# Block-sparse attention and a squared-ReLU MLP on one core: when six weight blocks are decoded, and how values and spilled outputs are laid out

## The chip, the cores and the metric

The kernel runs on one core of a Trainium2 chip. The metric is the device time of one execution in microseconds. Work is spread over TensorE (PE; its weight loads are shown apart as PEld), VectorE (DVE), ScalarE (ACT), GpSimd (POOL) and SyncE (SP), which here only issues transfers. Each engine takes its instructions in the order in which they were written for it and waits by semaphores for the others.

## The reference

`q`, `k` and `v` are 4 batches × 8 heads × 768 positions × 64 features in float32. Attention is masked by blocks of 32 positions, and its output is the input of an MLP over all 3072 tokens:

```python
scores = scale * np.matmul(q, k.transpose(0, 1, 3, 2))
mask = np.abs(blk_i - blk_j) <= window              # window = 1, blocks of 32
mask = mask | (blk_i == 0) | (blk_j == 0) | (blk_i == n_blocks - 1) | (blk_j == n_blocks - 1)
for qb in range(n_blocks):
    for kb in sampled_blocks[qb]:                   # 3 random blocks per row of blocks
        mask[qb * block:(qb + 1) * block, kb * block:(kb + 1) * block] = True
scores = np.where(mask, scores, -1000000000.0)
attn = np.exp(scores - np.max(scores, axis=-1, keepdims=True))
attn = attn / (np.sum(attn, axis=-1, keepdims=True) + 1e-09)
x = np.matmul(attn, v)                              # then heads side by side: 3072 x 512
h = x @ w_in                                        # 512 x 2048
r = np.maximum(h, 0.0)
out = (s * (r * r) + b) @ w_out                     # 2048 x 512
```

The weights reach the device as raw 64-bit words, so the kernel turns each of them into two float32 parts itself.

## The kernel before, in words

Attention goes slot by slot. A dense slot (`aD0` to `dD1` in the list `ORD`) is the first and last block of queries of one batch for four heads: two units of work. A sparse slot (`0A1` to `1C6`, 44 of them) is one row of blocks of a *pair* of batches for all heads: four units. The pairs are batches 0 and 1, called a and b, and batches 2 and 3, called c and d. There are 52 slots and N = 192 units. Units 0 to 99 are almost all of the first pair, 100 to 191 almost all of the second. Per unit PE forms scores (L914 dense, L936 sparse), DVE takes the maximum (L953), ACT the exponential (L965), PE transposes (L990), DVE or ACT copies the result out of PSUM (L1001, L1003), PE multiplies with the values (L1022 dense, L1033 sparse), DVE scales (L1039), PE transposes again (L1045), ACT copies (L1050), and SP spills the slot's output to a DRAM tensor `xd` (L1057 sparse, L1061 dense). On PE the scores of a slot stand two slots ahead of its product with the values.

Keys of a pair lie in one large tile (`kt0`, `kt1`); POOL copies the blocks that a sparse slot needs into `kk` (L873 to L886). Values of sparse slots are loaded by SP, slot by slot, into `vA` and `vB` (L765 window, L858 sampled). Values of dense slots are loaded by `load_v` into tiles `z0` and `z1`: 128 columns of all 768 rows of a batch per load, two loads a slot, 16 in all (L729). Afterwards `z0` and `z1` hold the split input of the MLP.

The 32 blocks of weights (16 of `w_in`, `i0` to `i15`, and 16 of `w_out`, `o0` to `o15`) go through the same decode, `decode_f64`: SP loads 512 KB into one of three staging buffers `kraw` (L57), DVE masks and combines (L75, L77, L78), ACT takes sign and magnitude (L79, L81, L82), and DVE writes the high part (L83) and the low part (L84, L85) where the block has its home. The homes of the first six blocks in the list `WL` (`i0 o0 i1 o1 i2 i3`) lie in `kt0`, the keys' tile of the first pair. The three staging buffers also take the MLP's first inputs, read back from `xd` by `xload` (L386) and split by ACT and DVE (`xsplit`, L399 and L401).

After attention come 30 plain MLP steps: `mlp1` (L426 to L428), `relu`, `square`, `hidden_high`, `hidden_low` (L431 to L447), `mlp2` (L468 to L470), each for a group of 384 tokens and one block of 128 hidden features. They run while the rest of the weights is decoded. Then the remaining batches use a scheme with seven products in place of eight (L605), for which DVE prepares sums of weights and inputs (L563 to L589).

The order of all this, up to the preparation of the seven products, is not written by hand. A class `Plan` holds every step with its engine, an assumed cost, what it depends on, which buffers it takes and uses, and a due number. `Plan.order` plays the engines forward in time: at each point the engine that can start earliest takes, among the steps that could start by then, the one with the smallest due number. Due numbers are in units of attention: a maximum of unit n has n - 26, a copy out of PSUM n - 8, the load of dense values u - 12 where u is the slot's first unit, loads of sampled values u - 13, a spill u - 14. The decode of the k-th block of `WL` has N + 22.5 + 15.5 k, that is 214.5, 230 and so on, its load 4 less, and the reload of the MLP's input N + 6: all of them above every due number of attention, so they are only taken where an engine had nothing of attention to do.

Of the kernel before, what the change touches and what calls it, by code (L numbers as in the profile page):

```python
# [9 lines left out]
F32 = mybir.dt.float32  # L10
# [9 lines left out]
P = 128  # L20
# [3 lines left out]
F64_SHIFT = 8.0 * 0x38000000  # L24
F32_MOST = float(0x7F7FF000)
T = {
# [176 lines left out]
def kernel(  # L203
# [16 lines left out]
    nc = tc.nc  # L220
    B, S, DM = v.shape
# [4 lines left out]
    BLK = 32  # L226
    NPAIR = 4
# [15 lines left out]
    dpool = ctx.enter_context(tc.tile_pool(name="dpool", bufs=1, space=DRAM))  # L243
# [4 lines left out]
    nc.gpsimd.memset(b_top, F32_MOST + F64_SHIFT)  # L248
    b_most = cpool.tile([P, 1], F32, name="b_most")
    nc.gpsimd.memset(b_most, F32_MOST)  # L250
    xd = dpool.tile([B, 2, P, NM, NPAIR, BLK], F32, name="xd")
    wod = dpool.tile([4, P, 2 * DM], F32, name="wod")


# [8 lines left out]
    NBANK = 7  # L263
    RB = 3
# [118 lines left out]

    def xload(g, c2, dst=None):
        t = scratch("kraw", 2 * HALF, f"xraw{g}_{c2}") if dst is None else dst
        nc.sync.dma_start(out=t.rearrange("p (t y) -> p t y", t=NM), in_=xd[g // 2, g % 2, :, :, 2 * c2:2 * c2 + 2, :].rearrange("p t c n -> p t (c n)"))  # L386
        xraw[(g, c2)] = t

    def xsplit(g, c, part=None):
# [259 lines left out]
    with ExitStack() as es:  # L649
        pers = es.enter_context(tc.tile_pool(name="pers", bufs=1))  # L650
        QB = 4
# [49 lines left out]

        vbox = {}

        def dense_values(n):
            if "z0" not in vbox:
                for z in ("z0", "z1"):
                    vbox[z] = gp.tile([P, 4, NCH, P], F32, tag=z, name=f"v{z}", bufs=1)
            return vbox[f"z{n // 4}"][:, n % 4]

        def value_tiles():  # L710
            if "A" not in vbox:
                for z in "AB":
# [7 lines left out]
            value_tiles()  # L720
            return vbox["B"][:, n - 1] if n else vbox["A"][:, NST]

        vst = {}

        def load_v(i, pr):
            kind, b, x, _ = slots[i]
            vt = vst[(i, pr)] = dense_values(len(vst) % 8)
            h0 = (2 * x + pr) * P
            nc.sync.dma_start(out=vt, in_=v[b, :, h0:h0 + P].rearrange("(c p) d -> p c d", p=P))  # L729

        def block_rows(e, j, n=1):

# [283 lines left out]

        def av_dense(i, j):

            xs, vt, pt = out_of(i, j), vst[(i, j)], pts_of.pop(unit_of[i] + j)
            for c in range(NCH):  # L1020
                for rows in halves:
                    nc.tensor.matmul(xs[rows], pt[c // 3][:, c % 3, rows], vt[:, c, rows], start=(c == 0), stop=(c == NCH - 1))  # L1022

        def av(i, j):
            kind, e, k, r = slots[i]
# [26 lines left out]
        def spill(i):  # L1052
            kind, b, k, _ = slots[i]
            xst = xst_of.pop(i)
            if kind == "s":
                hf, m = divmod(k - 1, NM)
                nc.sync.dma_start(out=xd[2 * b:2 * b + 2, hf, :, m].rearrange("a p c n -> p a (c n)"), in_=xst)  # L1057
                return
            x = k
            for m in range(2):  # L1060
                nc.sync.dma_start(out=xd[b, 1, :, NM - 2 + m, 2 * x:2 * x + 2, :],  # L1061
                                  in_=xst.rearrange("p x (a m n) -> p (x a) m n", a=2, m=2)[:, :, m, :])


        plan = Plan({"kraw": RB, "qr": QB, "dv": 8, "z0": 1, "z1": 1, "kk": 1, "kg": KG, "vs": VG, "vg": 2, "B": NBANK,
                     "o": 1, "P": len(ptiles), "pt": 5, "xst": 3, "xss": 2, "nm": 10, "dn": 5,
                     "rc": 5, "wp": 4, **{f"kt{k}": 1 for k in range(B // 2)}})
        op = plan.op
# [45 lines left out]


        pq = pdv = pvl = pvs = pk = o_m = o_e = o_rc = o_ev = None
        spills, tensor, lqs, before, globs = {}, {}, {}, {}, []

        costs = {"s": (530, 470, 265), "d": (810, 350, 780)}
        cols = {"s": (1800, 1024, 500), "d": (1536, 768, 768)}  # L1120
        for i, (kind, e, k, r) in enumerate(slots):
# [4 lines left out]
            if qk not in lqs:  # L1126
                lqs[qk] = {}
                for a in range(2):
                    for par in range(2):
# [4 lines left out]
            lv, av_deps, av_use, s_deps, s_use = {}, [], [], [], [("qr", qk)]  # L1134
            if dense:
                for pr in range(2):
                    new = [] if pdv else [("z0", "dv"), ("z1", "dv")]
                    pdv = lv[pr] = op("s", 450, u + pr - T["DL"], lambda i=i, pr=pr: load_v(i, pr), alloc=[("dv", (i, pr)), *new],
                                      use=[] if new else [("z0", "dv"), ("z1", "dv")], order=[pdv], nbytes=393e3)
                av_use = [("z0", "dv"), ("z1", "dv")]  # L1140
                s_use.append((f"kt{e // 2}", e // 2))
            else:
                prev = before.get(r)
                entire = k == STREAMS[r]
                first = not before
                blocks = [*range(k - 1, k + 2), 0] if entire else [k + 1]
                new = [("kk", "kk")] if first else []
                pk = op("g", 1900 if entire else 430, u - T["GK"], lambda i=i, w=entire: window_k(i, w),
                        [*parts_of(e, blocks), *(prev[0] if prev else [])], alloc=new, use=[(f"kt{e}", e)] + ([] if first else [("kk", "kk")]), order=[pk])
                s_deps.append(pk)  # L1150
                for a in range(NSL):
                    pk = op("g", 430 if a else 700, u - T["GK"] + 0.1 * (a + 1), lambda i=i, a=a: sampled_k(i, a), [o_si, *parts_of(e, range(NB))],
                            alloc=[] if a else [("kg", i)], use=[(f"kt{e}", e), ("kk", "kk")] + ([("kg", i)] if a else []), order=[pk])
                    s_deps.append(pk)
                s_use += [("kk", "kk"), ("kg", i)]

                vt = [("vg", "vA"), ("vg", "vB")]
                if first:
                    for m in range(5):
                        pvl = op("s", 450, u - T["VL"] - 0.5 + 0.1 * m, lambda m=m: global_values(m), alloc=[] if m else vt, use=vt if m else [],  # L1160
                                 order=[pvl], nbytes=(131e3 if m == 4 else 200e3))
                        globs.append(pvl)
                av_deps += globs if e == 0 else []
                for m in range(len(runs(k, entire)) + (entire and e > 0)):
                    pvl = op("s", 450, u - T["VL"] + 0.1 * m, lambda i=i, w=entire, m=m: window_v(i, w, m), prev[1] if prev else [],
                             use=vt, order=[pvl], nbytes=131e3)
# [50 lines left out]
            for j in range(nu):  # L1217
                pts = [("pt", (u + j, g)) for g in range(2)] if dense else [("pt", (u + j // 2 * 2, 0))]
                o = op("p", cost[2], u, lambda i=i, j=j: av(i, j), cols=col[2],
                       deps=[*evs[j], *av_deps, *([lv[j]] if dense else [])],  # L1220
                       alloc=[] if j else [("o", i)],
                       use=[*av_use, *pts] + ([("o", i)] if j else []) + ([("dv", (i, j))] if dense else []))
# [256 lines left out]
```

## Time and profile before

| | us |
|---|---|
| median of 3 runs | 800.08 (799.3 to 804.42) |
| profiled execution, time | 797.14 |
| its span, first to last instruction | 795.4 |
| PE busy | 729.3 (92% of the span) |
| DVE busy | 574.0 (72%) |
| ACT busy | 473.0 (59%) |
| POOL busy | 239.5 (30%) |

The profile is of one execution. Its times count from the first instruction. A busy PE means that a matmul is under way, not that the array is at its peak. "Granted clock" is the share of full speed that TensorE's clock had. Attention ends at about 258 us, the plain MLP steps and the decode of weights last until about 430 us, and the seven-product stage fills the rest.

### The profile page before, as it was taken

To read this page: it belongs to the slowest core of one execution; us is meant where nothing else is said; L and a number is where in the kernel's file an instruction comes from. 1 tells how busy PE (TensorE), PEld (TensorE's weight loads), DVE (VectorE), ACT (ScalarE), POOL (GpSimd) and SP (SyncE) were. 2 spreads that over 40 slices of the span, in tenths; PEclk is the share of its full clock that TensorE was granted. 3 is DMA by queue.
4 is the path that set the end of the run, shared out by engine and by line. 5 is a ranking of instruction groups with operands and counts; after the bars stand their busy time and mean duration, and the time that the engine had idled before them with its cause. 6 is when DMAs were issued, how large, how long until landed. Compare 5 with 4: busy or idle time off the path is not lost.

```text
span 795.4 us, 20754 instructions
## 1 busy us (share of the span) xinstructions
PE 729.3 (92%) x7872; PEld 618.5 (78%) x7872; DVE 574.0 (72%) x1439; ACT 473.0 (59%) x1141; POOL 239.5 (30%) x392
## 2 busy tenths in 40 slices
PE   6678779888889999999889999999999999999997
PEld 5456557666657897888778998998999998989996
DVE  3365667568568899998898678678668778766662
ACT  3365667567678787778874434476455357534542
POOL 6452533453531222221002322232232223222321
PEclk9799999889899999999999999999999999999999
DMA  9978789988787433544542241035000013000002
GB/s 253 241 175 228 206 238 234 242 239 209 179 229 196 141 123 105 170 160 131 137 139 75 87 125 56 33 80 149 12 1 0 1 40 99 1 1 1 1 0 80
DMA packets 118915, 95.80 MB, mean 120 GB/s; under 512 B 50272, under 2 KB 97504, under 8 KB 118816
## 3 DMA queue, kind: packets, MB, share of 16 engines
q1 hardware_dynamic: 116512, 88.18, 40.0%
q0 software_dynamic: 2304, 6.29, 3.1%
q8 instruction: 62, 1.02, 0.6%
q14 instruction: 37, 0.30, 0.1%
HBM read 75.57 MB, written 14.68 MB: 113 GB/s over the span
## 4 chain that ended last, share of the span: by engine, by line
PE 63%; DVE 15%; ACT 8%; DMA 6%; issue 5%; SPq 3%; ACTq 0%; DVEq 0%
PE m L605 19%; PE o L469 8%; PE o L470 8%; PE o L468 8%; PE t L990 6%; PE xs L1033 5%; PE s L936 4%; DMA vA<-in_v_dram 3%; DMA xd<-xst 2%; PE xs L1022 1%; DVE hid L438 1%; DMA qr_0d<-in_q_edge_dram 1%; DVE wkhp L84 1%; PE s L914 1%; ACT hid L442 1%
## 5 line engine op out<-in xcount | busy, mean ns | idle before, releaser
L447 POOL TENSOR_TENSOR hid<-hid,hid 128x384 fp32r<-128x384 f32 x120 | 132.7, 1106 | 410.1 <-ACT hid L623 246.1
L622 ACT ACTIVATE hid<-hid,sb_b,sb_s 128x384 f32<-128x384 f32 x96 | 68.1, 709 | 150.5 <-DVE hid L616 150.5
L965 ACT ACTIVATE ptile<-ptile,nm 128x256 f32<-128x256 f32 (+1 forms) x208 | 107.3, 518 | 46.6 <-DVE nm L953 46.2
L953 DVE CUSTOM_DVE_ANT_1 ptile<-s,mt 128x256 f32<-128x256 f32 x176 | 64.3, 421 | 30.4 <-PE s L936 30.3
L1033 PE MATMUL xs<-vA,pt 128*32 128x64 f32 x1696 | 50.3, 227 | 24.8 <-DMA vA<-in_v_dram 10.9
L1033 PEld LDWEIGHTS xs<-vA,pt 128*32 128x32 f32 x1696 | 37.4, 113 | 45.3 <-issue 13.0
L469 PE MATMUL o<-woutr,hid 128*128 128x512 f32 x168 | 66.9, 398 | 1.0 <-DVE woutr L85 1.0
L468 PE MATMUL o<-woutr,hid 128*128 128x512 f32 x168 | 65.9, 392 | 1.6 <-DVE woutr L83 1.6
L470 PE MATMUL o<-woutr,hid 128*128 128x512 f32 x168 | 66.8, 398 | 0.0
L605 PE MATMUL m<-wout,win 128*128 128x384 f32 x264 | 62.6, 340 | 2.5 <-ACT xrest L1372 1.6
L990 PE MATMUL t<-ident,ptile 128*128 128x128 f32 x448 | 64.2, 290 | 0.4 <-issue 0.4
L605 PE MATMUL m<-xp,wop 128*128 128x384 f32 x288 | 58.3, 337 | 0.0
L469 PE MATMUL o<-win,hid 128*128 128x512 f32 x144 | 56.8, 394 | 0.0
L616 DVE SCALAR_TENSOR_TENSOR hid<-hid 128x384 f32<-128x384 f32 x96 | 54.0, 563 | 3.3
L605 PE MATMUL m<-xp,win 128*128 128x384 f32 x288 | 55.1, 338 | 1.4 <-DVE xp L589 0.7
L990 PEld LDWEIGHTS t<-ident,ptile 128*128 128x128 f32 x448 | 51.2, 147 | 6.6 <-issue 1.7
L605 PEld LDWEIGHTS m<-xp,win 128*128 128x128 f32 x288 | 51.0, 188 | 4.6 <-DVE xp L589 1.2
L623 ACT CAST hid<-hid 128x384 fp32r<-128x384 f32 x96 | 49.4, 515 | 7.5 <-ACT hid L622 0.4
L886 POOL COPY kk<-kt 128x256 f32 x132 | 47.9, 402 | 18.8 <-issue 14.0
L605 PEld LDWEIGHTS m<-xp,wop 128*128 128x128 f32 x288 | 51.5, 188 | 2.1
L605 PEld LDWEIGHTS m<-wout,win 128*128 128x128 f32 x264 | 47.4, 188 | 5.5 <-ACT xrest L1372 2.4
L470 PE MATMUL o<-win,hid 128*128 128x512 f32 x126 | 49.8, 395 | 0.0
(172 smaller groups left out, 1778.4 us busy)
## 6 DMA issues: line engine op xcount, KB each, us to landing
vB<-in_v_dram SPq DMA_DIRECT2D x109, 128.0 KB, 3.6
vA<-in_v_dram SPq DMA_DIRECT2D x75, 128.0 KB, 4.5
raw_i<-in_w_in_dram SPq DMA_DIRECT2D x16, 512.0 KB, 4.0
raw_o<-in_w_out_dram SPq DMA_DIRECT2D x16, 512.0 KB, 3.7
vz<-in_v_dram SPq DMA_DIRECT2D x16, 384.0 KB, 6.2
xd<-xst SPq DMA_DIRECT2D x44, 128.0 KB, 3.8
out_dram<-ob SPq DMA_DIRECT2D x20, 256.0 KB, 2.0
sum<-xd SPq DMA_DIRECT2D x12, 384.0 KB, 4.5
```

The costliest lines, as they stand in the source:

```text
L447: (eng or nc.vector).tensor_tensor(out=htile(5 + i % 3), in0=t, in1=gh.bitcast(F32), op=ALU.subtract)
L468: nc.tensor.matmul(acc, gh[:, tsl], wout(f, 0), start=first, stop=False)
L469: nc.tensor.matmul(acc, gh[:, tsl], wout(f, 1), start=False, stop=False)
L470: nc.tensor.matmul(acc, gl[:, tsl], wout(f, 0), start=False, stop=last)
L605: nc.tensor.matmul(to, w_, x_, start=(c == 0 and k == 0), stop=(c == 1 and k == 2))
L616: vec.scalar_tensor_tensor(out=t, in0=t, scalar=0.0, in1=t, op0=ALU.max, op1=ALU.mult)
L622: nc.scalar.activation(t, t, AF.Identity, bias=sb_b, scale=sb_s)
L623: nc.scalar.copy(gh, t)
L953: nc.vector.tensor_tensor_reduce(out=pt, in0=sp, in1=msk, scale=-scale, scalar=FMAX if g == 0 else nm[:, 0:1], op0=ALU.add, op1=ALU.min, a ...
L965: nc.scalar.activation(pt[:, :w], pt[:, :w], AF.Exp, bias=nms[n][:, last:last + 1], scale=-1.0, accum_out=dns[i][:, g, j:j + 1])
L990: nc.tensor.transpose(tp[:, (2 * j + c) * P:(2 * j + c + 1) * P], src[:, c * P:(c + 1) * P], ident)
L1033: nc.tensor.matmul(xs[quads[pair]], pt[:, c, quads[pair]], vt[:, a, col:col + D], start=(j == 0 and c == 0), stop=(c == 1), tile_position= ...
```

## The change

Four things in the text of the kernel:

- **Weights.** Two new numbers, `WE` = -84 and `WD` = 16. The first six blocks of `WL` get the due number N - 84 + 16 k where that is smaller, that is 108, 124, 140, 156, 172 and 188 instead of 214.5 to 292; their loads have 4 less, as before. The other 26 blocks keep theirs. The steps themselves and their places in memory stay.
- **Dense values.** `load_v` now loads half the rows of a batch, all 512 columns of them, in one transfer of 768 KB whose rows are 2 KB long; two such loads a batch, eight in all instead of 16 of 384 KB with rows of 512 bytes. Batches a and c use `z0`, b and d `z1`, where before eight smaller pieces were spread over both. Both loads have the due number of the batch's first slot, and every product of the batch waits for both.
- **Spills.** `xd` gets another shape, so that the outputs of both batches of a pair stand side by side in it: a sparse spill writes runs of 1 KB instead of two runs of 512 bytes. What reads `xd` back (`xload`) has its addresses changed to match, with runs of the same length as before.
- **First order.** The list `ORD` itself is the same in both kernels. The order in which steps stand on the engines changes only as `Plan` works it out anew from the new due numbers, buffers and sizes.

```diff
-    "WL": "i0 o0 i1 o1 ...", "WP": 22.5, "WS": 15.5, "XP": 16.0, "LOW": 24,
+    "WL": "i0 o0 i1 o1 ...", "WP": 22.5, "WS": 15.5, "WE": -84.0, "WD": 16.0, "XP": 16.0, "LOW": 24,
...
-    xd = dpool.tile([B, 2, P, NM, NPAIR, BLK], F32, name="xd")
+    xd = dpool.tile([B // 2, 2, P, NM, 2, NPAIR, BLK], F32, name="xd")
...
-        def load_v(i, pr):
-            kind, b, x, _ = slots[i]
-            vt = vst[(i, pr)] = dense_values(len(vst) % 8)
-            h0 = (2 * x + pr) * P
-            nc.sync.dma_start(out=vt, in_=v[b, :, h0:h0 + P].rearrange("(c p) d -> p c d", p=P))
+        def load_v(b, half):
+            if ("d", b) not in vbox:
+                vbox[("d", b)] = gp.tile([P, NCH, DM], F32, tag=f"z{b % 2}", name=f"vz{b}", bufs=1)
+            rows, n = slice(half * HALF, (half + 1) * HALF), NCH // 2
+            nc.sync.dma_start(out=vbox[("d", b)][:, half * n:(half + 1) * n], in_=v[b, rows, :].rearrange("(c p) d -> p c d", p=P))
...
-                nc.sync.dma_start(out=xd[2 * b:2 * b + 2, hf, :, m].rearrange("a p c n -> p a (c n)"), in_=xst)
+                nc.sync.dma_start(out=xd[b, hf, :, m].rearrange("p a c n -> p a (c n)"), in_=xst)
...
+                vz = (f"z{e % 2}", ("dv", e))
+                if e not in dvs:
+                    dvs[e] = []
+                    for half in range(2):
+                        pdv = op("s", 450, u - T["DL"] + 0.1 * half, lambda e=e, half=half: load_v(e, half), alloc=[] if half else [vz],
+                                 use=[vz] if half else [], order=[pdv], nbytes=786e3)
+                        dvs[e].append(pdv)
+                av_deps += dvs[e]
+                av_use = [vz]
...
+            wat = N + min(T["WP"] + T["WS"] * k, T["WE"] + T["WD"] * k if k < 6 else 1e9)
...
-            pw = last_load = op("s", 450, N + T["WP"] - 4 + T["WS"] * k, load, [prev_k], alloc=[raw], nbytes=524e3, late=T["LATE"])
+            pw = last_load = op("s", 450, wat - 4, load, [prev_k], alloc=[raw], nbytes=524e3, late=T["LATE"])
...
-                mine[m] = wdone[(which, f, m)] = op(eng, cost[m], N + T["WP"] + T["WS"] * k + 0.3 * m, fn, deps, alloc=alloc, order=order,
+                mine[m] = wdone[(which, f, m)] = op(eng, cost[m], wat + 0.3 * m, fn, deps, alloc=alloc, order=order,
```

More of the change, by code (lines that the diff above doesn't have):

```diff
@@ L385, in xload @@
         t = scratch("kraw", 2 * HALF, f"xraw{g}_{c2}") if dst is None else dst
-        nc.sync.dma_start(out=t.rearrange("p (t y) -> p t y", t=NM), in_=xd[g // 2, g % 2, :, :, 2 * c2:2 * c2 + 2, :].rearrange("p t c n -> p t (c n)"))
+        nc.sync.dma_start(out=t.rearrange("p (t y) -> p t y", t=NM), in_=xd[g // 4, g % 2, :, :, g // 2 % 2, 2 * c2:2 * c2 + 2, :].rearrange("p t c n -> p t (c n)"))
         xraw[(g, c2)] = t
@@ L702 @@
         vbox = {}
[L704 to L708, printed above, removed]
         def value_tiles():
@@ L721, in sampled_values @@
             return vbox["B"][:, n - 1] if n else vbox["A"][:, NST]
-        vst = {}
-        def load_v(i, pr):
-            kind, b, x, _ = slots[i]
-            vt = vst[(i, pr)] = dense_values(len(vst) % 8)
-            h0 = (2 * x + pr) * P
-            nc.sync.dma_start(out=vt, in_=v[b, :, h0:h0 + P].rearrange("(c p) d -> p c d", p=P))
+        def load_v(b, half):
[3 more added lines that the diff above has]
+            nc.sync.dma_start(out=vbox[("d", b)][:, half * n:(half + 1) * n], in_=v[b, rows, :].rearrange("(c p) d -> p c d", p=P))
         def block_rows(e, j, n=1):
@@ L1017, in av_dense @@
         def av_dense(i, j):
-            xs, vt, pt = out_of(i, j), vst[(i, j)], pts_of.pop(unit_of[i] + j)
+            _, b, x, _ = slots[i]
+            xs, vt, pt = out_of(i, j), vbox[("d", b)], pts_of.pop(unit_of[i] + j)
             for c in range(NCH):
                 for rows in halves:
-                    nc.tensor.matmul(xs[rows], pt[c // 3][:, c % 3, rows], vt[:, c, rows], start=(c == 0), stop=(c == NCH - 1))
+                    nc.tensor.matmul(xs[rows], pt[c // 3][:, c % 3, rows], vt[:, c, (2 * x + j) * P + rows.start:(2 * x + j) * P + rows.stop], start=(c == 0), stop=(c == NCH - 1))
         def av(i, j):
@@ L1060, in spill @@
             for m in range(2):
-                nc.sync.dma_start(out=xd[b, 1, :, NM - 2 + m, 2 * x:2 * x + 2, :],
+                nc.sync.dma_start(out=xd[b // 2, 1, :, NM - 2 + m, b % 2, 2 * x:2 * x + 2, :],
                                   in_=xst.rearrange("p x (a m n) -> p (x a) m n", a=2, m=2)[:, :, m, :])
-        plan = Plan({"kraw": RB, "qr": QB, "dv": 8, "z0": 1, "z1": 1, "kk": 1, "kg": KG, "vs": VG, "vg": 2, "B": NBANK,
+        plan = Plan({"kraw": RB, "qr": QB, "z0": 1, "z1": 1, "kk": 1, "kg": KG, "vs": VG, "vg": 2, "B": NBANK,
                      "o": 1, "P": len(ptiles), "pt": 5, "xst": 3, "xss": 2, "nm": 10, "dn": 5,
@@ L1116 @@
         pq = pdv = pvl = pvs = pk = o_m = o_e = o_rc = o_ev = None
-        spills, tensor, lqs, before, globs = {}, {}, {}, {}, []
+        spills, tensor, lqs, before, globs, dvs = {}, {}, {}, {}, [], {}
         costs = {"s": (530, 470, 265), "d": (810, 350, 780)}
@@ L1133 @@
                         lqs[qk].setdefault(a, []).append(pq)
-            lv, av_deps, av_use, s_deps, s_use = {}, [], [], [], [("qr", qk)]
+            av_deps, av_use, s_deps, s_use = [], [], [], [("qr", qk)]
             if dense:
[L1136 to L1140, printed above, removed]
+                vz = (f"z{e % 2}", ("dv", e))
[7 more added lines that the diff above has]
+                av_use = [vz]
                 s_use.append((f"kt{e // 2}", e // 2))
@@ L1219 @@
                 o = op("p", cost[2], u, lambda i=i, j=j: av(i, j), cols=col[2],
-                       deps=[*evs[j], *av_deps, *([lv[j]] if dense else [])],
+                       deps=[*evs[j], *av_deps],
                        alloc=[] if j else [("o", i)],
-                       use=[*av_use, *pts] + ([("o", i)] if j else []) + ([("dv", (i, j))] if dense else []))
+                       use=[*av_use, *pts] + ([("o", i)] if j else []))
                 a_ops.append(o)
```

2 rows, old and new, of the table T are left out of this document.

## The prediction, made before the changed kernel was run

> **What bounds the kernel now.** I read the table of stretches first, cut where the kernel changes its work: attention of the second pair (140 to 258 us), then the plain MLP in which the weights are decoded (258 to 430), after which PE is busy 360 of 366 us and nothing is to be had. The columns are the stretch, its length, busy time of PE, PEld, DVE, ACT and POOL with counts, PE's granted clock, the DMA engines' share and GB/s.
>
> ```profile
> 140.00:180.00 40.00, 33.86 (x711) 24.81 (x716) 24.06 (x94) 24.96 (x78) 17.45 (x41) 0.83 0.93 240
> 180.00:258.00 78.00, 66.45 (x1954) 49.65 (x1939) 57.36 (x235) 58.09 (x198) 26.22 (x68) 0.96 0.77 202
> 258.00:300.00 42.00, 41.31 (x273) 37.48 (x271) 38.42 (x65) 32.82 (x60) 11.50 (x10) 1.00 0.43 131
> 300.00:380.00 80.00, 74.03 (x364) 64.82 (x364) 73.22 (x123) 62.43 (x110) 15.72 (x14) 1.00 0.44 138
> 380.00:430.00 50.00, 43.78 (x201) 36.77 (x200) 45.47 (x84) 34.31 (x63) 6.01 (x5) 0.97 0.48 134
> 430.00:796.00 366.00, 360.41 (x1783) 322.83 (x1782) 255.71 (x518) 180.39 (x370) 99.43 (x92) 1.00 0.14 43
> ```
>
> From 258 to 430 PE stands idle 0.69 + 5.97 + 6.22 = 12.88 us while DVE is busy 157.1 of 172 us (91%). Next the chain of waits, once for the second pair's attention, once for the MLP stage:
>
> ```profile
> by line: PE t L990 22.4%; PE xs L1033 19.0%; PE s L936 17.3%; DMA vA<-in_v_dram 10.6%; issue 6.2%; PE xs L1022 6.0%; PE xs L1045 4.5%; DMA xd<-xst 3.5%; DVE ptile L953 3.0%; PE s L914 2.5%; ACT ptile L965 1.6%; ACT xst L1050 1.2%; DVE xss L
> ```
>
> ```profile
> by line: issue 7.9%; DVE hid L438 5.6%; DVE wkhp L84 5.4%; ACT hid L442 5.2%; DVE win L85 4.7%; DVE wklp L78 4.5%; PE m L605 4.1%; DVE wout L85 3.4%; ACT hid L431 3.4%; DVE wkhp L75 3.3%; DVE win L83 3.1%; PE o L469 2.8%; DVE wout L83 2.7%;
> ```
>
> The two stages have different bounds. In attention PE's own lines carry 72% of the chain and transfers 14%; DVE and ACT carry about 6%. In the MLP stage the chain runs through DVE, mostly the decode's lines 75 to 85. What PE waits for there (engine and line, releaser, us in all, times, longest):
>
> ```profile
> PE h L428 <- DVE win L85: 4.8, 6, 1.3
> PE o L468 <- DVE woutr L83: 1.6, 1, 1.6
> PE m L605 <- ACT xrest L1372: 1.6, 2, 1.0
> PE xs L1033 <- ACT xst L1050: 1.2, 2, 0.7
> PE o L469 <- DVE wout L85: 1.0, 1, 1.0
> PE o L469 <- DVE woutr L85: 1.0, 2, 0.7
> ```
>
> 4.8 + 1.6 + 1.0 + 1.0 = 8.4 us are waits for a decoded block; the rest of the 12.9 is mostly preparation of the seven-product stage (L1372 and its like), which queues on DVE behind the last decodes.
>
> **Part 1, the six blocks.** One block's decode on DVE and ACT (min/median/max ns, first and last start; the last two rows, a view by groups, have busy us and mean ns):
>
> ```profile
> L75 DVE TENSOR_SCALAR wkhp<-raw_i x16: 396/419/423, 171.7 to 382.2; 128x512 int32<-128x512 int32 x16
> L77 DVE TENSOR_SCALAR wklp<-raw_i x16: 415/420/1237, 172.0 to 382.5; 128x512 int32<-128x512 int32 x16
> L79 ACT ACTIVATE raw_i<-raw_i x16: 660/668/729, 172.5 to 383.3; 128x512 f32<-128x512 f32 x16
> L78 DVE SCALAR_TENSOR_TENSOR wklp<-wklp,raw_i x16: 679/690/1532, 175.9 to 382.9; 128x512 f32<-128x512 int32 x16
> L83 DVE TENSOR_TENSOR win<-wkhp,raw_i x14: 673/684/784, 182.1 to 387.9; 128x512 fp32r<-128x512 f32 x14
> ```
>
> ```profile
> L84 DVE TENSOR_SCALAR wkhp<-win x17: 396/427/1129, 184.0 to 395.9; 128x512 int32<-128x512 int32 x17
> ```
>
> ```profile
> L85 DVE SCALAR_TENSOR_TENSOR win<-wklp,wkhp x17: 659/692/1553, 189.5 to 396.4; 128x512 fp32r<-128x512 f32 x17
> ```
>
> ```profile
> L82 ACT ACTIVATE wkhp<-wkhp,b_most 128x512 int32<-128x512 f32 x31 | 22.2, 717 | 0.4
> L81 ACT ACTIVATE wkhp<-wkhp,b_top 128x512 f32<-128x512 int32 x30 | 21.6, 719 | 5.9 <-DVE wkhp L75 5.6
> ```
>
> DVE: 0.419 + 0.420 + 0.690 + 0.684 + 0.427 + 0.692 = 3.33 us a block; ACT: 0.668 + 0.717 + 0.719 = 2.10 us. Before, one block alone gets as far as L83 ahead of 257 us, as the groups of 140 to 257 us show:
>
> ```profile
> L83 DVE TENSOR_TENSOR win<-wkhp,raw_i 128x512 fp32r<-128x512 f32 x1 | 0.8, 784 | 0.0
> ```
>
> So five blocks really move: 16.7 us of DVE and 10.5 us of ACT leave the MLP stage and enter attention. The loads, before 258 us:
>
> ```profile
> L57 SPq DMA_DIRECT2D raw_i<-in_w_in_dram x2: 419/423/427, 164.2 to 250.0; - x2
> L57 SPq DMA_DIRECT2D raw_o<-in_w_out_dram x2: 381/402/422, 231.5 to 256.6; - x2
> ```
>
> Four are issued already (the last at 256.6), so some three more 512 KB loads fall into attention, and three come earlier within it.
>
> *What it takes away.* With 16.7 us less to do, DVE runs five blocks ahead of PE, more than the 8.4 us of decode waits; these go whole. Of the other 4.5 us I take 1.6: the preparation starts earlier, but after it DVE's sums are still in a row on DVE and PE's own pace becomes what is next. Gain 10.0 us; bounds 8.4 and 12.9.
>
> *What it costs on DVE and ACT in attention.* 27.2 us of work join a stage whose chain is 6% DVE and ACT. At that share it costs 27.2 × 0.06 = 1.6 us; if every DVE step stood in front of a step that PE awaits, 16.7 us. The cover is idle DVE time. With four of the five blocks between 180 and 258, DVE would be busy 57.36 + 13.3 = 70.7 of 78 us, 91%. At exactly that share (38.42 of 42) PE between 258 and 300 still ran 41.31 of 42 us. But attention hands on from PE to DVE to ACT to PE more often than the MLP, and both engines take their instructions in the written order, so a 0.7 us step ahead of a maximum (L953) delays the exponential, the transposes and the values' product behind it. I take 3.5 us, double the share of today and near the lower end, because DVE there waits for PE more than PE for DVE.
>
> The decode's operands lie beside POOL's: row L77 is 420 ns at the median but 1237 at most, L85 692 and 1553, and between 180 and 258 POOL is busy 26.22 of 78 us. [...]
>
> *What the loads cost.* Each is issued by SP in front of value loads. The nearest row is the same with a smaller load: SP issues an x load (384 KB) and window values right behind it, and the chain holds their landing:
>
> ```profile
> 203.90 0.54 SPq L386 DMA_DIRECT2D xraw<-xd  x1
> ```
>
> ```profile
> 204.53 7.59 DMA vA<-in_v_dram
> ```
>
> where a vA load lands in 4.5 us at the median (rows below): 3.1 us late. Three more loads would cost 9.3 us if each hit like this; nothing if they go into the free 23% of the DMA engines (180 to 258: share 0.77; 18 us free, while 3 × 524 KB at 202 GB/s need 7.8). From the fourth load on SP also has to wait for a staging buffer, which comes free with L83 of an earlier block; behind it stand the value loads of the next slots, which PE awaits, and the spills, which ACT's copies await. That costs nothing as long as DVE gets to L83 in time, and it is in the same bounds. I take 0.5 us each, 1.5 us, nearer to nothing, since two of the loads of today fall in this stage without such a link in the chain.
>
> **Part 2, values and spills.** Landing times (KB each, median us):
>
> ```profile
> vA<-in_v_dram SPq DMA_DIRECT2D x75, 128.0 KB, 4.5
> ...
> vz<-in_v_dram SPq DMA_DIRECT2D x16, 384.0 KB, 6.2
> xd<-xst SPq DMA_DIRECT2D x44, 128.0 KB, 3.8
> ...
> kt<-in_k_blk_dram SPq DMA_DIRECT2D x8, 384.0 KB, 6.3
> kt<-in_k_blk_dram SPq DMA_DIRECT2D x4, 768.0 KB, 7.9
> ```
>
> Sixteen dense value loads of 512-byte runs become eight of 768 KB in 2 KB runs, the same 6.3 MB. The nearest rows are the keys: 384 KB in 512-byte runs land in 6.3 us, 768 KB in 1 KB runs in 7.9, though at different times. By them two old loads (12.4 us in a row) become one of about 8, and up to a third of the queue's time is saved; at the other end nothing is, and a first product, which needed two of the old loads, now needs the whole batch: 0.79 MB more, at 240 GB/s 3.3 us, for batches c and d. For a that costs nothing, since the product comes after the next slot's scores and these wait for their queries:
>
> ```profile
> 26.41 3.50 PE L914 MATMUL s<-kt,qr_0d 64*64 64x384 f32 x16 [9.74 <-DMA qr_0d<-in_q_edge_dram]
> ```
>
> The bytes in front of those queries stay the same, so a better rate would show here. Spills keep their 128 KB, in 1 KB instead of 512-byte runs; 3.5% of 128 us of chain (4.5 us) waits for them, of which I take 0.5 off. With 0.5 for the values (ends: -4, +6.6): -1.0 us. [...]
>
> **The sum.** -10.0 + 3.5 + 1.5 - 1.0 = -6.0 us. The profiled execution took 797.1 us (span 795.4), which gives 791.1; the median of the runs is 800.1, three above, so 794.1, and I say 794. Its own range: gain 8.4 to 12.9 and costs 1 to 7 give 788 to 799.
>
> **Rivals.**
>
> *Attention takes it all for nothing* (chance 0.22). DVE's waits hide the whole decode and the longer runs pay: 800.1 - 12.9 - 1.5 = 785.7. For it: PE and transfers are 86% of attention's chain. Against: DVE at 91% there.
>
> *The blocks are not early* (0.13). Raw weights and x share three staging buffers, and the splits of x hold them today until just before the MLP's start:
>
> ```profile
> L401 DVE TENSOR_TENSOR xp<-xraw,xp x8: 527/544/559, 193.1 to 255.7; 128x384 fp32r<-128x384 f32 x8
> ```
>
> If weights and x queue for each other, either fewer than six are decoded by the end, or x comes last and the first product at 260 waits for it. What is gained in decode waits is paid at the boundary: 800, within 3.
>
> *Value loads come late behind the weights* (0.20): the mechanism that ends slower. SP's one queue carries six 512 KB loads among 128 KB loads that the slot needs at once; five of them new in place. At 3.1 us each, as at 204.5, they cost 15.5 us, with DVE's 3.5: 800.1 - 10 + 19 - 1 = 808. It ends above the old time from (10 + 1 - 3.5) / 5 = 1.5 us per load. For it: DMA share 0.93 from 140 to 180, with a granted clock of 0.83 there. Against: share 0.77 afterwards.
>
> **Numbers.** Forecast 0.45, rivals 0.22, 0.13, 0.20. A change under 1% (8 us) can hardly be told from none. Below 792.1 lie nearly all of the second case and 0.2 of the first: 0.40. Above 808.1 lie a good half of the last and a little of the third: 0.14. The rest, 0.46, is within 1%. The range 785 to 807 leaves out about 0.08 below and 0.12 above.
>
> **What would show it.** In the changed profile: six loads of weights before attention ends, L83 and L85 six times by then (fewer: third case); PE's waits for decoded blocks between attention and the seven products near 0 instead of 8.4, PE's idle there 3 us instead of 12.9; attention's end 3 to 5 us later than 258; DVE's share in its last 78 us near 90%; no vA link of 7 us right behind a load of weights (else the last case); vz in eight loads of 8 us. The forecast is wrong if attention ends more than 8 us later or not later at all, or if PE keeps its waits for decode in the MLP stage.

## The result

The changed kernel takes 787.4 us (median of 4 runs, 785.7 to 790.8) against 799.7 us before (4 runs, 797.6 to 804.4). The ratio is 0.9885, with a 95% interval of 0.9845 to 0.9926; a second measurement of both gave 0.9875 (0.9811 to 0.9939). By the ratios it is faster, by about 1.2%, or 9 to 10 us; the medians themselves lie 12.3 us apart here and 7.6 us in the second measurement (797.8 and 790.2). The profiled execution took 788.3 us (span 786.5), 8.9 us less than the profiled one of before.

Here is the table of stretches of the changed kernel, cut and with columns as before (busy time of PE, PEld, DVE, ACT, POOL, granted clock, DMA share, GB/s):

```profile
140.00:180.00 40.00, 30.38 (x753) 22.49 (x753) 24.48 (x95) 25.20 (x79) 16.48 (x40) 0.91 0.84 224
180.00:258.00 78.00, 65.47 (x1897) 46.09 (x1896) 64.77 (x248) 62.27 (x200) 27.22 (x68) 0.98 0.73 203
258.00:300.00 42.00, 41.33 (x293) 37.24 (x283) 36.24 (x64) 31.28 (x63) 11.10 (x10) 1.00 0.44 129
300.00:380.00 80.00, 80.00 (x402) 72.46 (x401) 76.46 (x126) 63.41 (x115) 18.48 (x15) 1.00 0.50 152
380.00:430.00 50.00, 44.57 (x210) 37.35 (x209) 44.32 (x83) 32.45 (x62) 8.57 (x7) 1.00 0.38 107
```

From 300 to 380 us PE now works without a gap; before, it stood idle 6 us there. From 380 to 430 it still loses 5.4 us. What PE waits for in the MLP stage, and the loads of weights before 258 us:

```profile
PE m L605 <- ACT xrest L1370: 1.6, 2, 1.0
PE m L605 <- ACT hid L431: 1.4, 1, 1.4
PE xs L1026 <- ACT xst L1043: 1.0, 2, 0.7
PE m L605 <- DVE xp L589: 0.7, 2, 0.4
PE m L605 <- DVE sum L1379: 0.7, 1, 0.7
PE o L469 <- DVE woutr L85: 0.7, 1, 0.7
```

```profile
L57 SPq DMA_DIRECT2D raw_i<-in_w_in_dram x4: 396/416/440, 164.5 to 214.7; - x4
...
L57 SPq DMA_DIRECT2D raw_o<-in_w_out_dram x2: 374/416/458, 175.6 to 188.2; - x2
```

The loads of all six blocks are issued by 215 us, and the 8.4 us of waits for decoded blocks have shrunk to 1.0 us (the row with L85, and one of 0.3 us). What is left is the preparation of the seven products. The two ends of the MLP stage can be read from two groups, the first plain product (L426) and the first of the seven products (L605); the last two numbers before the semicolon are first and last start. First of before, then of after:

```profile
L426 PE MATMUL h<-xp,win x112: 333/334/522, 260.3 to 400.1; 128*128 128x384 f32 x112
...
L605 PE MATMUL m<-wout,win x264: 333/339/442, 402.7 to 773.7; 128*128 128x384 f32 x132
```

```profile
L426 PE MATMUL h<-xp,win x112: 333/334/440, 259.3 to 390.7; 128*128 128x384 f32 x112
...
L605 PE MATMUL m<-wout,win x264: 333/338/447, 393.3 to 764.8; 128*128 128x384 f32 x132
```

The stage takes 402.7 - 260.3 = 142.4 us before and 393.3 - 259.3 = 134.0 us after. That is 8.4 us, as much as the waits for decode, but the two are not the same microseconds. The rows of just these two stretches, before and after, show that:

```profile
260.30:402.70 142.40, 133.91 (x661) 118.58 (x657) 129.27 (x221) 108.86 (x192) 27.23 (x24) 0.99 0.47 139
```

```profile
259.30:393.30 134.00, 132.32 (x723) 118.79 (x721) 123.25 (x209) 102.34 (x188) 29.57 (x24) 1.00 0.50 147
```

PE's idle time falls by 6.8 us, from 8.5 to 1.7, and the counts differ: after, the first plain product stands ahead of attention's last product with the values. Its 64 matmuls (L1026), from 260.3 to 261.4 us, are counted to the MLP stage here, 1.3 us with the wait in front of them. Without them the MLP stage is some 9.7 us shorter. Part of this is the clock: before, the stage held one stretch at a lower clock (0.83 on average from 390 to 400 us), after, none.

So the first plain product starts 1.0 us earlier only because of its place in the order. Attention, which now holds more decodes, ends about 0.3 us later by this account; its last transpose starts at 262.9 us instead of 261.6. The rest of the kernel is 0.5 us longer. 0.3 - 9.7 + 0.5 = -8.9, as between the two profiled executions.

Attention did not get its extra work for nothing. This is what PE waits for from 130 to 258 us after the change:

```profile
PE xs L1038 <- DVE xss L1032: 9.4, 10, 2.0
PE xs L1026 <- ACT ptile L957: 8.7, 1, 8.7
PE xs L1026 <- issue: 2.0, 3, 1.1
PE xs L1026 <- ACT xst L1043: 1.9, 2, 1.2
```

The first row has grown. PE's second transpose of a slot waits for DVE's scaling of the output, ten times, 9.4 us in all; before, the same wait (L1045 behind L1039) came three times in this stretch, 1.0 us in all:

```profile
PE xs L1045 <- DVE xss L1039: 1.0, 3, 0.3
```

DVE's order around the longest of the ten shows why:

```profile
207.10 0.69 DVE L993 COPY pt<-t 128x512 f32<-128x512 f32 x1 [0.15 <-PE t L982]
207.71 0.81 DVE L83 TENSOR_TENSOR win<-wkhp,raw_i 128x512 fp32r<-128x512 f32 x1
208.45 0.36 DVE L968 TENSOR_SCALAR rc<-dn 128x4 f32<-128x4 f32 x1
208.84 0.18 DVE L969 RECIPROCAL rc<-rc 128x4 f32<-128x4 f32 x1
209.05 0.42 DVE L1032 TENSOR_TENSOR xss<-xs,rc 128x256 f32<-128x256 f32 x1
```

A decode step (L83) stands ahead of the reciprocal and the scaling (L1032) for which PE is waiting. At the next longest ones, ending at 183.8, 228.2 and 245.3 us, a step of the decode (L83 or L85) stands there too.

Other things make up for it in these two profiles. PE's waits for value loads, 5.1 us in this stretch before, are gone from the list. And the granted clock was higher: by the tables, the clock withheld in the 118 us from 140 to 258 comes to 40 × 0.17 + 78 × 0.04 = 9.9 us before and 40 × 0.09 + 78 × 0.02 = 5.2 us after. Which part of the change did this is not shown.

### The profile page after: what moved, and what is told of

It is laid out like the page before. It is cut to its first block, busy times and chain, and to the rows that moved or that the text cites. A ratio compares the mean times of both kernels' runs of the same rounds, so it can differ in the third digit from the quotient of the medians.

```text
span 786.5 us, 20729 instructions
## 1 busy us (share of the span) xinstructions
PE 722.4 (92%) x7872; PEld 611.4 (78%) x7872; DVE 576.2 (73%) x1439; ACT 470.3 (60%) x1141; POOL 243.2 (31%) x392
## 4 chain that ended last, share of the span: by engine, by line
PE 56%; DVE 18%; ACT 7%; DMA 7%; issue 6%; SPq 5%; POOL 0%; ACTq 0%; DVEq 0%; POOLq 0%
PE m L605 19%; PE o L470 8%; PE o L469 8%; PE o L468 8%; PE xs L1026 4%; PE s L928 4%; PE t L982 4%; DMA vA<-in_v_dram 2%; DMA xd<-xst 2%; DVE wklp L78 1%; DVE wkhp L75 1%; DVE ptile L945 1%; SPq L850 1%; DMA qr_0d<-in_q_edge_dram 1%; DVE hid L438 1%
## 5 line engine op out<-in xcount | busy, mean ns | idle before, releaser
L447 POOL TENSOR_TENSOR hid<-hid,hid 128x384 fp32r<-128x384 f32 x120 | 135.1, 1127 | 399.1 <-ACT hid L623 249.0
L1026 PEld LDWEIGHTS xs<-vA,pt 128*32 128x32 f32 x1696 | 36.5, 112 | 45.3 <-issue 16.1
L1026 PE MATMUL xs<-vA,pt 128*32 128x64 f32 x1696 | 49.6, 226 | 23.2 <-ACT ptile L957 8.7
L605 PE MATMUL m<-wout,win 128*128 128x384 f32 x264 | 62.6, 340 | 3.0 <-ACT xrest L1370 1.6
L605 PE MATMUL m<-xp,wop 128*128 128x384 f32 x288 | 58.3, 337 | 0.0
L605 PE MATMUL m<-xp,win 128*128 128x384 f32 x288 | 55.1, 338 | 1.4 <-DVE xp L589 0.7
L982 PEld LDWEIGHTS t<-ident,ptile 128*128 128x128 f32 x448 | 48.7, 142 | 8.9 <-ACT ptile L957 2.8
L605 PEld LDWEIGHTS m<-xp,win 128*128 128x128 f32 x288 | 50.9, 188 | 4.6 <-DVE xp L589 1.2
L605 PEld LDWEIGHTS m<-xp,wop 128*128 128x128 f32 x288 | 51.5, 188 | 2.1
L605 PEld LDWEIGHTS m<-wout,win 128*128 128x128 f32 x264 | 47.4, 188 | 6.0 <-ACT xrest L1370 2.4
```

What stands on the lines that cost most here:

```text
L447: (eng or nc.vector).tensor_tensor(out=htile(5 + i % 3), in0=t, in1=gh.bitcast(F32), op=ALU.subtract)
L605: nc.tensor.matmul(to, w_, x_, start=(c == 0 and k == 0), stop=(c == 1 and k == 2))
L982: nc.tensor.transpose(tp[:, (2 * j + c) * P:(2 * j + c + 1) * P], src[:, c * P:(c + 1) * P], ident)
L1026: nc.tensor.matmul(xs[quads[pair]], pt[:, c, quads[pair]], vt[:, a, col:col + D], start=(j == 0 and c == 0), stop=(c == 1), tile_position= ...
```

## The experiments

Theory A was that the gain is the decode that leaves the MLP stage. Theory B was that the longer runs of values and spills made it. Four kernels undo the change in parts. All ratios below are to the kernel before on the same chip.

**The weights alone.** The kernel before, with only the new due numbers (the line that sets them; it is used in two others):

```diff
+            wat = N + min(T["WP"] + T["WS"] * k, T["WE"] + T["WD"] * k if k < 6 else 1e9)
```

> Only the due numbers of the first six weight blocks are changed; dense values and spills as before. Theory A (the decode that leaves the MLP stage is the gain): the stretch from attention's last transpose to the first of the seven products shrinks by 9 to 11 us, as it did in the changed kernel (261.5 to 402.7 before, 262.7 to 393.3 after), PE's waits for decoded blocks fall from 8.4 to about 1 us, attention ends 1 to 4 us later; 792 to 794 against 800. Theory B (the longer runs of values and spills made the gain, in the order of transfers): 798 to 802.

Measured: 792.6 us, ratio 0.9916 (0.9885 to 0.9946). Theory A's number. The two rows of its profile:

```profile
L426 PE MATMUL h<-xp,win x112: 333/334/443, 265.2 to 395.6; 128*128 128x384 f32 x112
...
L605 PE MATMUL m<-wout,win x264: 333/339/446, 398.2 to 769.6; 128*128 128x384 f32 x132
```

The MLP stage takes 133.0 us instead of 142.4, and it starts 4.9 us later. PE's waits for decoded blocks are 2.1 us.

**Values and spills alone.** The changed kernel with `WE` so large that all weights keep their old due numbers:

```diff
-    ... "WE": -84.0, ...
+    ... "WE": 9e9, ...
```

> Values as whole rows and spills side by side, but all weights with their old due numbers. Theory A: the MLP stage keeps its 8.4 us of waits for decoded blocks; attention ends within 3 us of the old end; 797 to 801 against 800. Theory B: 788 to 792.

Measured: 798.5 us, ratio 1.0014 (0.9977 to 1.0051): no change. Its two rows, and PE's longest waits in the MLP stage:

```profile
L426 PE MATMUL h<-xp,win x112: 333/334/522, 258.5 to 402.6; 128*128 128x384 f32 x112
...
L605 PE MATMUL m<-wout,win x264: 333/338/446, 405.2 to 774.9; 128*128 128x384 f32 x132
```

```profile
PE o L468 <- DVE win L83: 5.1, 1, 5.1
PE h L428 <- DVE win L85: 2.9, 5, 1.1
PE o L468 <- DVE woutr L83: 1.5, 1, 1.5
```

In this execution attention ends a little earlier, and the MLP stage is longer, 146.7 us. Whatever the layout saves in attention, PE then waits for decode: its first `mlp2` alone stands 5.1 us for block o0.

**Values alone, and spills alone.** The kernel before with `load_v` in whole rows; the kernel before with the new shape of `xd`:

```diff
+            nc.sync.dma_start(out=vbox[("d", b)][:, half * n:(half + 1) * n], in_=v[b, rows, :].rearrange("(c p) d -> p c d", p=P))
```

> Values as whole rows alone, spills and weights as before. Both theories: 2.8 us earlier up to the first sparse slots (the changed kernel shows that lead from slot 0A1 on), and lost again where batch c's first product waits for its whole batch (slot cD0, lead 0.1 us in the changed kernel). Theory A: 798 to 802. Theory B: some 4 us off 800, the rest being the spills.

```diff
+    xd = dpool.tile([B // 2, 2, P, NM, 2, NPAIR, BLK], F32, name="xd")
```

> Spills side by side alone. The landing of a 128 KB spill goes from 3.8 to 3.6 us as in the changed kernel, and ACT's waits for spills between 130 and 258 us (7.1 us before) shrink by less than 1 us. Theory A: 799 to 801. Theory B: about 796.

Measured: values alone 801.5 us, 1.0041 (1.0006 to 1.0075); spills alone 798.9 us, 1.0008 (0.9968 to 1.0048). Neither makes it faster. The values' kernel starts its MLP stage at 256.1 us, 4.2 us earlier than before, and the stage then takes 145.8 us: the same give-back as above. (That profiled execution was the fastest of its ten, 796.6 us, so the early start says little; the wait of `mlp2` for block o0 is again 5.1 us.) Theory B is out.

**The changed kernel again, and the values of c and d earlier.** In the profile of after PE stands still for 8.7 us up to 162.4 (second row of its waits above). Batch d's two loads are issued at 145 us, and the chain of waits holds, behind them, a spill:

```profile
145.45 7.72 DMA vz<-in_v_dram
153.24 6.55 DMA xd<-xst
```

One kernel repeats the changed one, the other loads c and d earlier:

```diff
-                        pdv = op("s", 450, u - T["DL"] + 0.1 * half, ...
+                        pdv = op("s", 450, u - (T["DL"] if e < 2 else 24) + 0.1 * half, ...
```

> The changed kernel once more, beside the three below. Theory A with an extra: the values and spills are worth nothing alone (798.5 to 801.5 in the runs so far) since the MLP stage then waits for decode, but some 2 to 4 us on top of the weights alone, since the decode no longer waits; 788 to 791. Rival: the parts simply add, and it is as the weights alone, 792 to 794.

> The changed kernel, with the value loads of batches c and d due 24 instead of 12 units ahead of their first slot. In the changed kernel PE stands still for 8.7 us up to 162.4; theory S: this comes from batch d's two 768 KB loads at 145 us, behind which a spill is issued at 153.2 and lands at 159.8, so that ACT's copy of the next output and the exponentials behind it wait. With the loads earlier the stall shrinks below 3 us and attention ends 2 to 5 us sooner, 784 to 787. Rival: the DMA engines are the bound between 120 and 180 us whatever the order; the stall moves to another place, 788 to 791.

Measured: the changed kernel 790.2 us, 0.9875 (0.9811 to 0.9939); with the earlier loads 799.1 us, 0.9990 (0.9948 to 1.0031). Loading earlier costs 9 us. In its profile the lag builds up from 110 to 150 us, and a stall of 6.3 us ends at 170 us, there behind a load of window values. What theory S forecast did not come, and the rival was too mild: the earlier loads made the kernel slower. What caused the stall of 8.7 us stays open. The repeat has 4.1 us of stall at that place instead of 8.7, with the same program; such single stalls differ from execution to execution.

**DVE's time doubled.** Five of the six DVE steps of the six blocks are done twice:

```diff
+            if k < 6:
+                st = [(eng, (lambda fn=fn: (fn(), fn())) if m in (0, 1, 6, 7, 8) else fn, needs) for m, (eng, fn, needs) in enumerate(st)]
```

> The changed kernel, in which five of the six DVE steps (L75, L77, L83, L84, L85) of the first six blocks are done twice, in the same place, with the same result: 6 x 2.64 = 15.9 us more of DVE in attention. If DVE time there is covered as in the prediction (3.5 us for 27.2 us of DVE and ACT work, 0.13 a us), attention ends 2 us later: 790 to 793. If DVE bounds attention by now, 10 to 16 us later: 798 to 806.

Measured: 800.6 us, 1.0007 (0.9974 to 1.0039), 10.4 us more than the changed kernel beside it. The expectation of 2 us is refuted. Up to the first decode this profile agrees with that of after within 2.4 us; from there the lag grows to 10.3 us at the first plain product (269.6 us). PE's largest wait from 166 to 262 us is the same as above, 12.3 us in all where the changed kernel has 8.8, first of this kernel, then of after:

```profile
PE xs L1038 <- DVE xss L1032: 12.3, 6, 3.0
```

```profile
PE xs L1038 <- DVE xss L1032: 8.8, 8, 2.0
```

Something else appears. Six stretches of 5 us, five in which this kernel runs at a lower clock and one (210 to 215) in which the changed kernel does, first of after, then of this kernel (the third number from the end is the granted clock):

```profile
185.00:190.00 5.00, 4.98 (x179) 3.46 (x171) 4.08 (x18) 3.75 (x10) 2.43 (x7) 1.00 0.71 207
195.00:200.00 5.00, 4.96 (x129) 3.65 (x118) 4.38 (x22) 3.88 (x15) 0.85 (x3) 1.00 0.95 265
210.00:215.00 5.00, 5.00 (x115) 3.27 (x122) 3.29 (x14) 3.30 (x12) 2.59 (x6) 0.70 0.77 211
215.00:220.00 5.00, 4.30 (x138) 2.92 (x127) 3.91 (x19) 3.43 (x13) 1.84 (x5) 1.00 1.00 255
225.00:230.00 5.00, 3.30 (x102) 2.27 (x93) 3.74 (x12) 3.21 (x12) 0.60 (x3) 1.00 0.67 186
235.00:240.00 5.00, 3.79 (x112) 2.84 (x111) 3.33 (x15) 4.61 (x17) 1.55 (x5) 1.00 0.76 235
```

```profile
185.00:190.00 5.00, 3.70 (x97) 2.22 (x97) 4.23 (x17) 2.35 (x9) 1.18 (x4) 0.66 0.75 226
195.00:200.00 5.00, 3.26 (x70) 1.71 (x74) 4.40 (x12) 1.86 (x7) 0.52 (x2) 0.66 0.70 213
210.00:215.00 5.00, 2.36 (x72) 1.70 (x72) 4.86 (x16) 3.87 (x13) 3.72 (x9) 1.00 0.73 190
215.00:220.00 5.00, 4.57 (x104) 3.70 (x105) 4.75 (x16) 2.50 (x10) 4.14 (x9) 0.69 0.90 234
225.00:230.00 5.00, 3.15 (x78) 2.94 (x71) 1.97 (x11) 2.59 (x7) 1.49 (x4) 0.71 0.64 186
235.00:240.00 5.00, 3.56 (x98) 2.39 (x98) 4.83 (x17) 2.22 (x9) 1.50 (x4) 0.74 0.63 168
```

The granted clock falls again and again: to between 0.66 and 0.74 in five of the six stretches. In the sixth, from 210 us, it is 1.00, PE is busy 2.36 of 5 us, and the next stretch has 0.69.

**The doubled time told to the planner.** The same kernel, with the doubled costs in the plan:

```diff
-                mine[m] = wdone[(which, f, m)] = op(eng, cost[m], wat + 0.3 * m, ...
+                mine[m] = wdone[(which, f, m)] = op(eng, cost[m] * (2 if k < 6 and m in (0, 1, 6, 7, 8) else 1), wat + 0.3 * m, ...
```

> The kernel with the doubled steps (15.9 us more DVE in attention; 800.6 against 790.2 for the changed kernel), but with the doubled costs told to the planner, so that it can put the steps elsewhere. If it is DVE's time itself that bounds attention, as much later as before, 798 to 803. If the harm of the doubled steps was their place, in front of steps that PE awaits, most of it goes: 790 to 795; this would fit that four blocks early are no faster than six.

Measured: 803.2 us, 1.0055 (1.0022 to 1.0088). No better than untold. So a wrong cost in the plan is not the reason; that no other order could hide the time is not shown. The same wait for the scaling takes 16.7 us between 166 and 262 us.

**More loads.** Behind each of the first six weight loads SP issues another copy of 512 KB:

```diff
+            if k < 6:
+                load = lambda load=load, k=k, f=f: (load(), nc.sync.dma_start(out=idle[k], in_=w_out[f * P:(f + 1) * P, :].bitcast(I32)))
```

> The changed kernel, in which SP issues behind each of the first six weight loads another copy of 512 KB, from DRAM to a DRAM tensor that nobody reads. At 0.5 us a load as predicted: 3 us later, 791 to 795. At 3.1 us a load, as in the rival by which value loads come late: 18 us, 805 to 811. An unused copy also writes 512 KB to DRAM, so this is an upper bound for a load's cost.

Measured: 794.7 us, 0.9943 (0.9910 to 0.9976), 4.5 us more than the changed kernel: 0.75 us a copy, and these also write. The rival's 3.1 us a load is refuted, the predicted 0.5 us is of the right size.

**Three and four blocks early.** The bound `k < 6` becomes `k < 3` and `k < 4`:

```diff
-            wat = N + min(..., T["WE"] + T["WD"] * k if k < 6 else 1e9)
+            wat = N + min(..., T["WE"] + T["WD"] * k if k < 4 else 1e9)
```

> The changed kernel with three blocks early instead of six; the other three keep their old due numbers. Theory C (the doubled steps showed 0.7 us of attention for each us of DVE, so the last blocks cost what the first did not): attention ends 4 to 7 us sooner than with six, and PE's waits for decoded blocks come back in part, 2 to 5 us; 787 to 793. If the blocks' cost in attention is small and even (0.13 a us of DVE), attention ends 1 to 2 us sooner and the waits come back as far: 790 to 795.

> The same with four blocks early. Theory C: attention 3 to 5 us sooner than with six, 1 to 2 us of waits back; 785 to 790, the best of the three. With an even small cost: 789 to 793.

Measured: three 790.1 us, 0.9905 (0.9874 to 0.9937); four 787.4 us, 0.9875 (0.9810 to 0.9939); six had 0.9885 and 0.9875. The MLP stage, from L426 to L605, takes 134.2 us with three and 134.6 with four, against 134.0 with six and 146.7 with none named early. So three early due numbers already remove most of the waits: PE's waits for decoded blocks are 2.0 us with three and 1.2 with four, against 1.0 with six. The return of 1 us is what a small and even cost would give, not the 2 to 5 us of theory C. (The stretches with four and six hold the 64 matmuls of attention, that with three does not.) Nor does attention end sooner: its last transpose starts at 262.9 us with four as with six. (The profiled execution with three was the slowest of its ten, 796.1 us, so its 268.5 says little.) Theory C, that the last blocks are dear, is not borne out and not refuted: the intervals of three, four and six overlap.

**Weights and values without the spills.**

```diff
-    xd = dpool.tile([B // 2, 2, P, NM, 2, NPAIR, BLK], F32, name="xd")
+    xd = dpool.tile([B, 2, P, NM, NPAIR, BLK], F32, name="xd")
```

> The changed kernel without the spills side by side (weights and values alone). If the spills are worth nothing, as alone (within 0.5% of before), the same as the changed kernel, 787 to 791. In the single profiles attention ended 2 us sooner with values alone than with both; if that holds, 785 to 788.

Measured: 790.5 us, 0.9918 (0.9876 to 0.9959), the same as the weights alone. Attention does not end sooner without the spills (first plain product at 262.1 us in its profile).

## Why the prediction was right, and where it was not

The sum said -6.0 us and 794; measured were 9 to 10 us by the ratios and medians of 787 and 790. Direction and cause hold, the size is short. In the profiles the missing 3 us lie in attention, which ended about 0.3 us later instead of 4.0 (3.5 + 1.5 - 1.0). Point by point:

- **The stage and its bound.** Right, and shown: the weights alone give 0.9916, where the whole change gave 0.9885 and 0.9875, and take 9.4 us off the MLP stage; the layout alone gives nothing, and in its profile that stage waits for decode.
- **What the MLP stage gains.** Predicted 10.0 us with bounds 8.4 and 12.9; measured 9.4 with the weights alone and, without attention's matmuls, some 9.7 with the whole change. The size was right; the way there only in part. The 8.4 us of decode waits went down to 1.0. The 1.6 us taken off the preparation of the seven products did not come: its waits (L1370, L589, L1379) stand in the profile of after as they stood before. PE's idle time from 258 to 430 is 6.1 us, not the 3 us named. What made up for it is less busy time, in part at a higher clock (1.00 from 380 to 430 us, where it was 0.97).
- **How many blocks it takes.** The text let five blocks move to remove 8.4 us. Fewer do. Before, two blocks, not one, are decoded when the first plain product starts at 260.3 us (the second between 258 and 260). With three named early four are, in a profile that reached that point late; the waits are then 2.0 us. Two blocks more are 6.7 us of DVE at 3.33 a block, near the 6.4 us of waits that go.
- **The cost on DVE and ACT, 3.5 us, and of the loads, 1.5 us.** Together 5.0 us, and the weights alone delay the first plain product by 4.9 us in one profiled execution; by the medians (799.1 and 792.6) the cost is 9.4 - 6.4 = 3.0. The size was about right. The reasoning was not: it took a rate of 0.06, doubled, from the share of the chain, and that rate fails as soon as it is used again. The next 15.9 us of DVE cost 10.4 us, 0.65 a us. A share of the chain says what the present work costs on average, not what the next microsecond costs. The predicted place was also wrong. I named the maximum (L953); the wait that came is PE's second transpose behind the scaling (L1039 before, L1032 after).
- **When attention ends.** Predicted 3 to 5 us later, and "not later at all" was named as a sign that the forecast is wrong. PE's last transpose of attention starts 1.3 us later (262.7 in the repeat), so that sign is narrowly absent, but the 3 to 5 us did not come either. The weights alone end 5.0 us later (266.6). The cost on DVE did come, 9.4 us of waits; the whole change made up for it, which the sum did not foresee.
- **DVE's share in the last 78 us.** Predicted near 90%, measured 64.77 of 78, 83%, because the eight splits of x moved behind 257 us. The first product did not wait for them, so the third rival did not occur.
- **GpSimd beside the decode.** The prediction set the long maxima of L77 and L85 (1237 and 1553 ns) beside POOL's work between 180 and 258 us. In the profile of before they do not lie there: of DVE's decode steps that start between 130 and 258 us none of 10 takes over 1 us, of those between 258 and 445 us 18 of 182 do. After the change it is none of 34 and 21 of 158: between 160 and 262 us the longest L83 is 811 ns against a median of 688, the longest L84 505 against 416, the longest L78 772 against 692, and all others are near their medians. Every one of the 18 and of the 21 overlaps a step of POOL's L447 (1127 ns on average after the change) by more than 0.1 us; of the shorter ones between 258 and 445 us 13 of 164 and 18 of 137 do. No run changes POOL's work, so that it makes these steps long is not shown.
- **Values and spills, -1.0 us.** This may be the term that was sized wrong, if the profiled executions are taken at their word: from the weights alone to the whole change the first of the seven products moves from 398.2 to 393.3, 4.9 us. By the ratios it is 0.9916 to 0.9885 or 0.9875, 2.5 to 3.3 us, with intervals that overlap, and weights with values but without spills give 0.9918. What the two layouts add beside the early weights is not settled. Alone they add nothing.
- **Rivals.** "Attention takes it all for nothing" comes nearest to the first median (785.7 against 787.4); by the ratios the forecast is nearer. As a mechanism it is wrong: PE waits 9.4 us for DVE's scaling in attention, where it waited 1.0 us before. "Value loads come late" is refuted by the doubled loads.

## What to carry to other kernels

Work taken off a bound stage is worth the waits for it and no more: read them by their releasers, and move only as many blocks as cover them. Time saved in front of a stage that is bound elsewhere is given back there, so an edit that shows nothing alone may count once the bound is gone, and is worth trying again then; whether values and spills do is not settled here. Idle time of an engine is a cover that is used up (here 15.9 us more of DVE's work cost 10.4 us): to price the next addition, add it twice, and do not go by the share of the chain.

## What the runs showed of the hardware

In the kernel with doubled DVE steps no stall of PE between 166 and 262 us is longer than 3.0 us, yet the mean granted clock over these 96 us is 0.89, against 0.98 in the changed kernel: 96 × 0.11 = 10.6 us withheld against 96 × 0.02 = 1.9.

What went ahead of a fall can be read from the profiles of before and after. Between 100 and 430 us the granted clock falls from 1.00 to 0.50 four times in the first and twice in the second, for 3.4 or 6.8 us. PE's busy share in the 3.41 us in front of each fall:

| profile | fall at, us | clock at 0.50 for, us | PE busy in the 3.41 us before |
|---|---|---|---|
| before | 147.8 | 6.8 | 44% |
| before | 161.5 | 6.8 | 43% |
| before | 209.2 | 6.8 | 50% |
| before | 393.6 | 3.4 | 33% |
| after | 158.4 | 6.8 | 0% |
| after | 209.6 | 3.4 | 40% |

The fall at 158.4 us comes within the stall of 8.7 us, the one at 209.6 right behind the 2.0 us that PE waited for DVE's scaling, the longest of the ten waits above. Cut from 100 to 430 us in the same steps of 3.41 us, the two profiles have 176 more stretches at full clock; in these PE was busy 51% or more, and the clock stayed. That is what two executions show; what sets the clock is not shown.

How much of the loss of the kernel with doubled steps is idle time and how much is busy time can be read from the stretch from 166 us to the first plain product, in which both kernels run almost the same number of matmuls, first the changed kernel, then the one with doubled steps:

```profile
166.00:259.30 93.30, 80.45 (x2260) 57.24 (x2258) 77.64 (x293) 75.40 (x240) 32.78 (x80) 0.98 0.73 203
```

```profile
166.00:269.60 103.60, 86.06 (x2259) 61.95 (x2257) 92.22 (x321) 76.38 (x240) 33.40 (x80) 0.90 0.64 182
```

Of the 10.3 us more, 5.6 are busy time of PE, at a mean granted clock of 0.90 against 0.98, and 4.7 are idle time, in this one pair of executions.

The same program differs from one profiled execution to another by several microseconds in attention: at the same place PE stood 8.7 us in one execution and 4.1 us in the other. Differences of that size between single profiles are no evidence; the medians and ratios are.
